# An mLSTM cell with a GELU block: three products of the cell as pairs of 64-column halves of the array

## The chip, the cores and the metric

The kernel runs on one core of a Trainium2 chip. The metric is the time of one execution on the device in microseconds (us), as the median of several runs. TensorE (PE in the profile) multiplies, its weight loads have a row of their own (PEld); VectorE is DVE, ScalarE is ACT, GpSimd is POOL, and SP issues the transfers.

## What is computed

A gated recurrent cell over 768 tokens for 4 batches of 8 heads, with keys, values and queries 40 wide, and behind it a feed-forward block with an exact GELU on all 3072 tokens. Everything is float32 except the two weight matrices, which come in float64.

```python
def _attn_ref(q, k, v, i_gate, f_gate, o_gate):      # (4, 8, 768, 40), gates (4, 8, 768)
    for t in range(S):
        m_new = np.maximum(f_gate[:, :, t] + m, i_gate[:, :, t])
        f_stab = np.exp(f_gate[:, :, t] + m - m_new)
        i_stab = np.exp(i_gate[:, :, t] - m_new)
        m = m_new
        C = f_stab[:, :, None, None] * C + i_stab[:, :, None, None] * np.einsum('bhd,bhe->bhde', vt, kt)
        n = f_stab[:, :, None] * n + i_stab[:, :, None] * kt
        h_tilde = np.einsum('bhde,bhe->bhd', C, qt)
        nq = np.einsum('bhd,bhd->bh', n, qt)[:, :, None]
        y[:, :, t] = 1.0 / (1.0 + np.exp(-o_gate[:, :, t])) * h_tilde / np.maximum(np.abs(nq), 1.0)

def _moe_ref(x, w_in, w_out):                        # x = y as (3072, 320), w_in (320, 2048), w_out (2048, 320)
    h = x @ w_in
    return 0.5 * h * (1.0 + erf(h / sqrt(2))) @ w_out
```

## The kernel before

The cell runs in six chunks of 128 tokens. Within a chunk the recurrence becomes products of matrices; a state (C with n as its 41st column) is carried from chunk to chunk. All the work of a chunk is done for each of the four batches b in turn, and one token lies on each partition.

The parts of the cell for one batch are four functions in `cell_steps`. `turn` (L268) transposes keys and queries, two heads at a time, into `pt` and copies them to `kT` and `qT`. Each of these holds pairs of heads: the first head of a pair in partitions 0 to 63, the second in 64 to 127. `scores` (L278) multiplies keys and queries of every head into `ps`, with the two heads of a pair in the two row halves of the array, and VectorE multiplies that by the weights W. From chunk 1 on it then reads the state: `pf` (L293) is one product for each of four pairs of heads, with `qT` (128 by 128 tokens) as the loaded operand and the state of the pair (82 columns) streamed. The state of a pair is block diagonal, so that one product serves both heads. VectorE scales it into `far`. Up to chunk 4 `scores` also updates the state: GpSimd weights the values (`vw`, L300), `pc` (L305) is one product for each pair with the keys of both heads loaded (128 columns) and the weighted values of both streamed (82 columns). Of its four blocks, head by head, only the two on the diagonal are used; GpSimd decays the state (L314) and VectorE adds those two blocks (L315). `values` (L317) multiplies W of each of eight heads (128 by 128, loaded) by its values and a column of ones (41, streamed) into `ph` (L321), adds `far`, and gates and divides the result on GpSimd and VectorE. `turn_y` (L337) transposes that through `px` into `xT`; its third transpose loads 64 columns.

The feed-forward block follows for all four batches of the chunk together: `up_steps` (L353) makes 16 pieces `pu` of 512 tokens, each from three products with 128, 128 and 64 rows, and `down_steps` (L363) sums 16 products into `po` for each batch.

The order of work on each engine is the order of the calls. `weave` spreads one list of steps between another. In chunk 0 the cell is woven with the conversion of `w_in` from float64 (ScalarE, GpSimd, VectorE); the up projection of chunk 0 is woven with that of `w_out`. Every later cell is woven with the down projection of the chunk before, four products of `po` after each step; the up projections stand alone. `activations` (exponentials and sigmoids on ScalarE) come ahead of each cell. The three products `pf`, `pc` and `ph` share two PSUM banks in turn (`ps_h`).

In the trace each float32 product appears as two weight loads and two matmuls, a transpose as one of each.

Of the kernel before, what the change touches and what calls it, by code (L numbers as in the profile page):

```python
# [9 lines left out]
F32 = mybir.dt.float32  # L10
U32 = mybir.dt.uint32
AF = mybir.ActivationFunctionType
OP = mybir.AluOpType

P = 128


# The upper halves of the float64 2^-126 and of the largest below 2^128, read as float32.
TINY = 3.4332275390625e-05
HUGE = 122879.9921875  # L20


def weave(main, fill):
    """Run the steps of main in order with those of fill spread evenly between them."""
    done = 0
    for n, step in enumerate(main):
        step()
        upto = len(fill) * (n + 1) // len(main)
        for f in fill[done:upto]:
            f()  # L30
        done = upto
    for f in fill[done:]:
        f()
# [3 lines left out]
def kernel(  # L37
# [9 lines left out]
    moe_w_out: bass.AP,  # L47
    out: bass.AP,
):
    # The cell in chunks of L tokens. With b_t the sum of f from the chunk's first token to t and  # L50
    # a_s = i_s - b_s, the stabiliser is m_t = b_t + M_t, M_t = max(m before the chunk, a_s for s <= t), and
    #   (C_t, n_t) = exp(m_before - M_t) (C, n)_before + sum over s <= t of exp(a_s - M_t) (v_s, 1) k_s^T.
    # Every exponent is at most 0, so this holds for gates of any size.
    nc = tc.nc

    B, H, S, D = q.shape
    L = P
    NCH = S // L
    NP = H // 2
    D1 = D + 1  # L60
# [23 lines left out]
    gates = gate_ctx.enter_context(tc.tile_pool(name="gates", bufs=1))  # L84
    ctx.enter_context(tc.manual_schedule())

    # ---- what stays: weights, state, load buffers with their constant parts
    w_in = const.tile([P, 3, DFF], F32, name="w_in")
    w_out = const.tile([P, NF, DM], F32, name="w_out")
    ident = const.tile([P, P], F32, name="ident")  # L90
# [13 lines left out]
    M_d = dram.tile([BH, S], F32, name="M_d")  # L104

    def load(n):
        """The inputs of token tile n (chunk n // B of batch n % B), one token a partition."""
        if n >= NCH * B:
            return
        c, b = divmod(n, B)  # L110
        for src, dst in ((q, qb), (k, kb), (v, vb), (o_gate, ob)):
            nc.sync.dma_start(out=dst[n % NLD][:, :, 0:D],
                              in_=src[b, :, c * L:(c + 1) * L, :].rearrange("h p d -> p h d"))
# [1 line left out]
    Mb, W = {}, {}  # L115

    def load_M(n):
        """M of token tile n on every partition."""
        if n >= NCH * B:
            return  # L120
        c, b = divmod(n, B)
        Mb[n] = wts.tile([P, H, L], F32, name="Mb", tag="Mb", bufs=NM)
        nc.sync.dma_start(out=Mb[n], in_=M_d[b * H:(b + 1) * H, c * L:(c + 1) * L]
                          .unsqueeze(0).to_broadcast([P, H, L]))
# [17 lines left out]
    for n in range(B):  # L142
        load(n)

    # ---- the gates, one row a head
    keep = gates.tile([BH, NCH, L], F32, name="keep")
    bl = gates.tile([BH, NCH, L], F32, name="bl")
    a = gates.tile([BH, NCH, L], F32, name="a")
# [34 lines left out]
    gate_ctx.close()  # L183
    gp = ctx.enter_context(tc.tile_pool(name="gp", bufs=1))

    # ---- the weights come in float64: the nearest float32, from the bits
    w_src = {}
    for name, w in (("in", moe_w_in), ("out", moe_w_out)):
        rows, cols = w.shape
# [1 line left out]
                              ap=[[2 * cols, rows], [1, 2 * cols]])  # L191

    def weight_steps():
        """What brings w_in and w_out in, a piece of at most WP columns a step."""
        pieces = []
        for f0 in range(0, DFF, WP):
            for cc, w in enumerate((P, P, KX)):
                pieces.append((w_src["in"][cc * P:cc * P + w, 2 * f0:2 * f0 + 2 * WP], w_in[0:w, cc, f0:f0 + WP]))
        n_in = len(pieces)
        for f in range(NF):  # L200
            pieces.append((w_src["out"][f * P:(f + 1) * P, :], w_out[:, f, :]))
        loaded = {}

        def fetch(i):
            if i < len(pieces):
                src, dst = pieces[i]
                w, n = dst.shape
                t = raw.tile([P, WP, 2], U32, name="bits", tag="bits")
                loaded[i] = t[0:w, 0:n, :]
                nc.sync.dma_start(out=loaded[i].rearrange("p n two -> p (n two)"), in_=src)  # L210

        def convert(i):
            dst = pieces[i][1]
            w, n = dst.shape
            x = loaded.pop(i)
            lo, hi = x[:, :, 0], x[:, :, 1]
            hf = hi.bitcast(F32)
            s = raw.tile([P, WP], F32, name="sig", tag="sig")[0:w, 0:n]
            p = raw.tile([P, WP], F32, name="pow", tag="pow")[0:w, 0:n]
            su, pu = s.bitcast(U32), p.bitcast(U32)  # L220
            # Into the range of float32: 0 below 2^-126, the end of the range from 2^128 on.
            nc.scalar.activation(out=s, in_=hf, func=AF.Abs)  # L222
            nc.gpsimd.tensor_scalar(out=s, in0=s, scalar1=TINY, scalar2=None, op0=OP.is_ge)  # L223
            nc.gpsimd.tensor_tensor(out=s, in0=s, in1=hf, op=OP.mult)  # L224
            nc.gpsimd.tensor_scalar(out=s, in0=s, scalar1=-HUGE, scalar2=HUGE, op0=OP.max, op1=OP.min)  # L225
            # The sign and the power of two, and the 53 bits of the significand rounded to 24.
            nc.vector.tensor_scalar(out=pu, in0=su, scalar1=3, scalar2=0x3F800000,  # L227
                                    op0=OP.logical_shift_left, op1=OP.bitwise_and)
            nc.vector.scalar_tensor_tensor(out=pu, in0=su, scalar=0xC0000000, in1=pu,
                                           op0=OP.bitwise_and, op1=OP.bitwise_or)  # L230
            nc.vector.tensor_scalar(out=su, in0=su, scalar1=0xFFFFF, scalar2=0x100000,
                                    op0=OP.bitwise_and, op1=OP.bitwise_or)
            nc.vector.scalar_tensor_tensor(out=s, in0=lo, scalar=2.0 ** -32, in1=su, op0=OP.mult, op1=OP.add)
            nc.vector.scalar_tensor_tensor(out=dst, in0=s, scalar=2.0 ** -20, in1=p, op0=OP.mult, op1=OP.mult)
            fetch(i + 2)

        fetch(0)
        fetch(1)
        steps = [lambda i=i: convert(i) for i in range(len(pieces))]
        return steps[:n_in], steps[n_in:]  # L240

    # ---- the cell
    def per_head(t, c, b):
        return t[:, c, b * H:(b + 1) * H].unsqueeze(2)

    def distances(c):
        """M_t - a_s for the chunk's weights exp(a_s - M_t); beyond the diagonal, what gives 0."""
        for b in range(B):
            n = c * B + b
            W[n] = wts.tile([P, H, L], F32, name="W", tag="W")  # L250
# [13 lines left out]

    def cell_steps(c):
        qT, kT, Pm, far, ys = {}, {}, {}, {}, {}

        def turn(b):  # L268
            n = c * B + b
# [8 lines left out]
        def scores(b):  # L278
            n = c * B + b
            Pm[b] = W.pop(n)  # L280
            # The heads of a pair run side by side in the array: each has its own bank.
            ps = [ps_sc.tile([P, NP, L], F32, name="ps", tag="sc") for hip in range(2)]
            for p in range(NP):
                for hip in range(2):
# [2 lines left out]
            for hip in range(2):  # L287
                w = Pm[b].rearrange("p (m two) t -> p m two t", two=2)[:, :, hip, :]
                nc.vector.tensor_tensor(out=w, in0=ps[hip], in1=w, op=OP.mult)  # L289
            if c > 0:  # L290
                pf = ps_h.tile([P, H, D1], F32, name="pf", tag="h")
                for p in range(NP):
                    nc.tensor.matmul(pf[:, 2 * p:2 * p + 2, :].rearrange("p h d -> p (h d)"), qT[b][:, p, :],  # L293
                                     state[b][:, p, :], start=True, stop=True)
                far[b] = two.tile([P, H, D1], F32, name="far", tag="far")
                nc.vector.tensor_tensor(out=far[b], in0=pf, in1=per_head(gT, c - 1, b).to_broadcast([P, H, D1]),
                                        op=OP.mult)
            if c + 1 < NCH:
                vw = two.tile([P, H, D1], F32, name="vw", tag="vw")
                nc.gpsimd.tensor_tensor(out=vw, in0=vb[n % NLD], in1=per_head(ewT, c, b).to_broadcast([P, H, D1]),  # L300
                                        op=OP.mult)
                pc = ps_h.tile([P, NP, 2 * D1], F32, name="pc", tag="h")
                for p in range(NP):
                    m = slice(2 * p, 2 * p + 2)
                    nc.tensor.matmul(pc[:, p, :], kb[n % NLD][:, m, :].rearrange("p h d -> p (h d)"),  # L305
                                     vw[:, m, :].rearrange("p h d -> p (h d)"), start=True, stop=True)
                for hip in range(2):
                    r, m = slice(DP * hip, DP * hip + DP), slice(D1 * hip, D1 * hip + D1)
                    st = state[b][r, :, m]
                    if c == 0:  # L310
                        nc.vector.tensor_copy(out=st, in_=pc[r, :, m])
                    else:
                        d = dec[r, c - 1, b * H:(b + 1) * H].rearrange("p (m two) -> p m two", two=2)[:, :, hip:hip + 1]
                        nc.gpsimd.tensor_tensor(out=st, in0=st, in1=d.to_broadcast([DP, NP, D1]), op=OP.mult)  # L314
                        nc.vector.tensor_tensor(out=st, in0=st, in1=pc[r, :, m], op=OP.add)  # L315

        def values(b):  # L317
            n = c * B + b
            ph = ps_h.tile([P, H, D1], F32, name="ph", tag="h")
            for h in range(H):  # L320
                nc.tensor.matmul(ph[:, h, :], Pm[b][:, h, :], vb[n % NLD][:, h, :], start=True, stop=True)  # L321
            hs = two.tile([P, H, D1], F32, name="hs", tag="hs")
            if c > 0:
                nc.vector.tensor_tensor(out=hs, in0=ph, in1=far[b], op=OP.add)  # L324
# [24 lines left out]
                    steps.append(lambda f=f, b=t - lag: f(b))  # L349
        return steps  # L350

    # ---- the feed-forward block, on the tokens of one chunk of every batch
    def up_steps(g):  # L353
        def step(f):
            m = slice(f * P, (f + 1) * P)
# [69 lines left out]
```

## Time and profile before

| what | value |
|---|---|
| time, median of 3 runs (lowest to highest) | 833.14 us (832.2 to 833.54) |
| span of the profiled execution, first to last instruction | 830.5 us |
| TensorE busy with matmuls | 674.7 us (81%) |
| weight loads | 394.8 us (48%) |
| VectorE busy | 240.7 us (29%) |
| GpSimd busy | 199.5 us (24%) |
| ScalarE busy | 170.4 us (21%) |

The profile gives the span of its execution alone; its whole time is not among the three runs, whose median lies 2.6 us above the span. Busy times overlap between engines. A busy TensorE is counted from the start of a matmul to its modelled end, so a stream of short matmuls looks busy while it waits for weight loads; how far the starts lie apart tells more.

### The profile page before, as it was taken

How to read it: one execution, taken by the hardware profiler on the slowest of the kernel's cores; microseconds unless marked ns; L12 is line 12 of the kernel's file. 1: busy time of each engine (PE TensorE's matmuls, PEld its weight loads, DVE VectorE, ACT ScalarE, POOL GpSimd, SP SyncE). 2: the span in 40 equal slices, each digit the busy share in tenths (PEclk: the TensorE clock that was granted, in tenths of full speed). 3: DMA queues.
4: the chain of work that ended last, by engine and by line, in shares of the span. 5: the costliest groups of instructions: out<-in, count | busy, mean ns of one | idle time of the engine just before them, and what ended most of it. 6: DMA issues, size and time to landing. Idle time of an engine off the chain costs nothing.

```text
span 830.5 us, 7094 instructions
## 1 busy us (share of the span) xinstructions
PE 674.7 (81%) x2714; PEld 394.8 (48%) x2714; DVE 240.7 (29%) x438; ACT 170.4 (21%) x288; POOL 199.5 (24%) x214
## 2 busy tenths in 40 slices
PE   2136424477579999799999799997999997999998
PEld 1125321122258733388533587333885335773365
DVE  4257554455534320034400144200344001330000
ACT  1411002111330022510223300225102234012200
POOL 2276654766612130011300021300113000000000
PEclk9975556788879999999999899998999998999999
DMA  9944371522204540024500035400221000000000
GB/s 141 248 80 95 66 120 29 148 64 63 63 9 66 79 110 0 0 41 66 133 23 1 6 64 82 109 0 1 41 40 41 1 0 9 9 17 0 0 9 24
DMA packets 132208, 43.47 MB, mean 52 GB/s; under 512 B 101104, under 2 KB 128752, under 8 KB 132176
## 3 DMA queue, kind: packets, MB, share of 16 engines
q1 hardware_dynamic: 132176, 43.04, 25.7%
q8 instruction: 21, 0.34, 0.2%
q14 instruction: 11, 0.09, 0.0%
HBM read 38.99 MB, written 4.03 MB: 52 GB/s over the span
## 4 chain that ended last, share of the span: by engine, by line
PE 67%; POOL 13%; issue 11%; ACT 5%; DVE 1%; DMA 1%; SPq 0%; POOLq 0%; ACTq 0%
PE pu L358 28%; PE po L371 25%; POOL sig L225 4%; PE ph L321 4%; POOL sig L223 4%; POOL sig L224 3%; PE ps L286 3%; PE pf L293 3%; ACT W L260 2%; PE pt L273 2%; PE pc L305 2%; POOL W L253 1%; ACT ob L263 1%; PE px L341 1%; ACT L263 1%
## 5 line engine op out<-in xcount | busy, mean ns | idle before, releaser
L358 PE MATMUL pu<-xT,w_in 128*128 128x512 f32 (+1 forms) x576 | 296.2, 646 | 36.4 <-ACT g L359 20.8
L371 PE MATMUL po<-w_out,g 128*128 128x320 f32 x768 | 228.5, 445 | 0.0
L358 PEld LDWEIGHTS pu<-xT,w_in 128*128 128x128 f32 (+1 forms) x576 | 96.6, 193 | 233.2 <-issue 189.8
L371 PEld LDWEIGHTS po<-w_out,g 128*128 128x128 f32 x768 | 143.6, 196 | 51.2 <-issue 5.0
L289 DVE TENSOR_TENSOR W<-ps,W 128x512 f32<-128x512 f32 x48 | 30.9, 685 | 293.5 <-PE ps L286 293.5
L359 ACT ACTIVATE g<-pu 128x512 f32<-128x512 f32 x96 | 57.1, 594 | 187.2 <-PE pu L358 187.2
L314 POOL TENSOR_TENSOR state<-state,dec 64x164 f32<-64x164 f32 x32 | 14.7, 461 | 241.5 <-PE pf L293 240.3
L273 PE MATMUL pt<-ident,kb 128*128 128x128 f32 x96 | 19.2, 335 | 60.5 <-ACT kT L276 60.5
L328 POOL TENSOR_TENSOR y<-hs,ob 128x320 f32<-128x320 f32 x24 | 19.3, 805 | 189.0 <-DVE hs L324 164.8
L321 PEld LDWEIGHTS ph<-vb,W 128*128 128x128 f32 x384 | 53.0, 215 | 4.0 <-PE px L341 0.8
L321 PE MATMUL ph<-vb,W 128*128 128x41 f32 x384 | 51.7, 300 | 0.4 <-PE px L341 0.4
L305 PE MATMUL pc<-vw,kb 128*128 128x82 f32 x160 | 24.9, 306 | 32.2 <-POOL vw L300 32.2
L253 POOL TENSOR_SCALAR_AFFINE_SELECT W<-W 128x1024 f32<-128x1024 f32 x24 | 37.2, 1571 | 56.9 <-DVE W L251 56.9
L273 PEld LDWEIGHTS pt<-ident,kb 128*128 128x128 f32 x96 | 14.1, 173 | 69.3 <-ACT kT L276 63.5
L223 POOL TENSOR_SCALAR sig<-sig 128x320 f32<-128x320 f32 (+2 forms) x28 | 34.8, 1243 | 47.0 <-ACT sig L222 47.0
L225 POOL TENSOR_SCALAR sig<-sig 128x320 f32<-128x320 f32 (+2 forms) x28 | 44.3, 1582 | 2.5
L251 DVE TENSOR_TENSOR W<-Mb,aT 128x1024 f32<-128x1024 f32 x24 | 33.3, 1425 | 26.0 <-DMA Mb<-M_d 26.0
L227 DVE TENSOR_SCALAR pow<-sig 128x320 uint32<-128x320 uint32 (+2 forms) x28 | 15.2, 543 | 86.3 <-POOL sig L225 86.2
L305 PEld LDWEIGHTS pc<-vw,kb 128*128 128x128 f32 x160 | 22.7, 219 | 33.3 <-POOL vw L300 33.3
L374 ACT COPY o_sb<-po 128x320 f32<-128x320 f32 x24 | 10.2, 425 | 132.3 <-PE po L371 132.3
L276 ACT COPY kT<-pt 128x512 f32<-128x512 f32 x24 | 13.9, 579 | 106.5 <-PE pt L273 106.5
L222 ACT ACTIVATE sig<-bits 128x320 f32<-128x320 f32 (+2 forms) x28 | 15.6, 563 | 97.4 <-DMA bits<-in_moe_w_out_dram 66.3
(71 smaller groups left out, 453.9 us busy)
## 6 DMA issues: line engine op xcount, KB each, us to landing
Mb<-M_d SPq DMA_DIRECT2D x24, 512.0 KB, 5.3
bits<-in_moe_w_out_dram SPq DMA_DIRECT2D x16, 320.0 KB, 2.9
bits<-in_moe_w_in_dram SPq DMA_DIRECT2D x8, 512.0 KB, 3.8
qb<-in_q_dram SPq DMA_DIRECT2D x24, 160.0 KB, 4.1
kb<-in_k_dram SPq DMA_DIRECT2D x24, 160.0 KB, 4.2
vb<-in_v_dram SPq DMA_DIRECT2D x24, 160.0 KB, 4.2
ob<-in_o_gate_dram SPq DMA_DIRECT2D x24, 160.0 KB, 3.8
out_dram<-o_sb SPq DMA_DIRECT2D x24, 160.0 KB, 1.9
```

What stands on the lines that cost most here:

```text
L223: nc.gpsimd.tensor_scalar(out=s, in0=s, scalar1=TINY, scalar2=None, op0=OP.is_ge)
L224: nc.gpsimd.tensor_tensor(out=s, in0=s, in1=hf, op=OP.mult)
L225: nc.gpsimd.tensor_scalar(out=s, in0=s, scalar1=-HUGE, scalar2=HUGE, op0=OP.max, op1=OP.min)
L251: nc.vector.tensor_tensor(out=W[n], in0=Mb.pop(n), in1=per_head(aT, c, b).to_broadcast([P, H, L]), op=OP.subtract)
L253: nc.gpsimd.affine_select(out=W[n], in_=W[n], compare_op=OP.is_ge, fill=1.0e4, base=0, pattern=[[0, H], [1, L]], channel_multiplier=-1)
L273: nc.tensor.transpose(pt[:, p, :], src[n % NLD][:, 2 * p:2 * p + 2, :].rearrange("p h d -> p (h d)"), ident)
L289: nc.vector.tensor_tensor(out=w, in0=ps[hip], in1=w, op=OP.mult)
L305: nc.tensor.matmul(pc[:, p, :], kb[n % NLD][:, m, :].rearrange("p h d -> p (h d)"), vw[:, m, :].rearrange("p h d -> p (h d)"), start=True, ...
L321: nc.tensor.matmul(ph[:, h, :], Pm[b][:, h, :], vb[n % NLD][:, h, :], start=True, stop=True)
L358: nc.tensor.matmul(pu, w_in[0:w, cc, m], xT[0:w, cc, :], start=(cc == 0), stop=(cc == 2))
L359: nc.scalar.activation(out=g[:, f, :], in_=pu, func=AF.Gelu)
L371: nc.tensor.matmul(po, g[:, f, b * L:(b + 1) * L], w_out[:, f, :], start=(f == 0), stop=(f == NF - 1))
```

## The change

The three products of the cell that load 128 columns are cut into halves of 64 columns. In the array each half has columns of its own, 0 to 63 or 64 to 127, and writes the same half of the partitions of its bank.

- `ph` (values): for each head two products, one for the first 64 tokens and one for the last 64; both stream the same 41 columns of values.
- `pf` (state read): for each pair of heads two products in the same way; both stream the same 82 columns of the state.
- `pc` (state update): for each pair one product a head, with the keys of that head loaded (64 columns) and the values of that head streamed (41 columns). The two blocks off the diagonal are no longer made, and the tile has 41 columns instead of 82.

The copies and sums that read `pc` read the whole half instead of a slice. Comments are left out below; the rest of the kernel is the same, five lines further down at the end.

```diff
@@ -264,6 +264,7 @@

     def cell_steps(c):
         qT, kT, Pm, far, ys = {}, {}, {}, {}, {}
+        halves = (slice(0, DP), slice(DP, P))

         def turn(b):
             n = c * B + b
@@ -278,7 +279,7 @@
         def scores(b):
             n = c * B + b
             Pm[b] = W.pop(n)
...
             ps = [ps_sc.tile([P, NP, L], F32, name="ps", tag="sc") for hip in range(2)]
             for p in range(NP):
                 for hip in range(2):
@@ -288,10 +289,12 @@
                 w = Pm[b].rearrange("p (m two) t -> p m two t", two=2)[:, :, hip, :]
                 nc.vector.tensor_tensor(out=w, in0=ps[hip], in1=w, op=OP.mult)
             if c > 0:
+
                 pf = ps_h.tile([P, H, D1], F32, name="pf", tag="h")
                 for p in range(NP):
-                    nc.tensor.matmul(pf[:, 2 * p:2 * p + 2, :].rearrange("p h d -> p (h d)"), qT[b][:, p, :],
-                                     state[b][:, p, :], start=True, stop=True)
+                    for r in halves:
+                        nc.tensor.matmul(pf[r, 2 * p:2 * p + 2, :].rearrange("p h d -> p (h d)"), qT[b][:, p, r],
+                                         state[b][:, p, :], start=True, stop=True)
                 far[b] = two.tile([P, H, D1], F32, name="far", tag="far")
                 nc.vector.tensor_tensor(out=far[b], in0=pf, in1=per_head(gT, c - 1, b).to_broadcast([P, H, D1]),
                                         op=OP.mult)
@@ -299,26 +302,28 @@
                 vw = two.tile([P, H, D1], F32, name="vw", tag="vw")
                 nc.gpsimd.tensor_tensor(out=vw, in0=vb[n % NLD], in1=per_head(ewT, c, b).to_broadcast([P, H, D1]),
                                         op=OP.mult)
-                pc = ps_h.tile([P, NP, 2 * D1], F32, name="pc", tag="h")
+
+                pc = ps_h.tile([P, NP, D1], F32, name="pc", tag="h")
                 for p in range(NP):
-                    m = slice(2 * p, 2 * p + 2)
-                    nc.tensor.matmul(pc[:, p, :], kb[n % NLD][:, m, :].rearrange("p h d -> p (h d)"),
-                                     vw[:, m, :].rearrange("p h d -> p (h d)"), start=True, stop=True)
+                    for hip in range(2):
+                        nc.tensor.matmul(pc[halves[hip], p, :], kb[n % NLD][:, 2 * p + hip, :], vw[:, 2 * p + hip, :],
+                                         start=True, stop=True)
                 for hip in range(2):
-                    r, m = slice(DP * hip, DP * hip + DP), slice(D1 * hip, D1 * hip + D1)
+                    r, m = halves[hip], slice(D1 * hip, D1 * hip + D1)
                     st = state[b][r, :, m]
                     if c == 0:
-                        nc.vector.tensor_copy(out=st, in_=pc[r, :, m])
+                        nc.vector.tensor_copy(out=st, in_=pc[r])
                     else:
                         d = dec[r, c - 1, b * H:(b + 1) * H].rearrange("p (m two) -> p m two", two=2)[:, :, hip:hip + 1]
                         nc.gpsimd.tensor_tensor(out=st, in0=st, in1=d.to_broadcast([DP, NP, D1]), op=OP.mult)
-                        nc.vector.tensor_tensor(out=st, in0=st, in1=pc[r, :, m], op=OP.add)
+                        nc.vector.tensor_tensor(out=st, in0=st, in1=pc[r], op=OP.add)

         def values(b):
             n = c * B + b
             ph = ps_h.tile([P, H, D1], F32, name="ph", tag="h")
             for h in range(H):
-                nc.tensor.matmul(ph[:, h, :], Pm[b][:, h, :], vb[n % NLD][:, h, :], start=True, stop=True)
+                for r in halves:
+                    nc.tensor.matmul(ph[r, h, :], Pm[b][:, h, r], vb[n % NLD][:, h, :], start=True, stop=True)
             hs = two.tile([P, H, D1], F32, name="hs", tag="hs")
             if c > 0:
                 nc.vector.tensor_tensor(out=hs, in0=ph, in1=far[b], op=OP.add)
```

On TensorE, one batch of chunk 1 from the scores to the values. `state_99` and `kb_113` are the state and the keys of a batch, `vb_118` the values of the one before. Before:

```order
L286 MATMUL ps<-qT,kT 128x128 x8
L293 MATMUL pf<-state_99,qT 128x82 x4
L305 MATMUL pc<-vw,kb_113 128x82 x4
L371 MATMUL po<-w_out,g 128x320 x4
L321 MATMUL ph<-vb_118,W 128x41 x8
L371 MATMUL po<-w_out,g 128x320 x4
```

And with the change:

```order
L287 MATMUL ps<-qT,kT 128x128 x8
L296 MATMUL pf<-state_99,qT 64x82 x8
L309 MATMUL pc<-vw,kb_113 64x41 x8
L376 MATMUL po<-w_out,g 128x320 x4
L326 MATMUL ph<-vb_118,W 64x41 x16
L376 MATMUL po<-w_out,g 128x320 x4
```

Nothing changes its place; each of the three groups has twice as many products that fill half the partitions. The instructions of the other engines stand in the same order with the same waits.

## Rows read from the trace of the kernel before

**Rows 1.** The page: the span, and each engine's busy time, share of span and instructions.

```profile
span 830.5 us, 7094 instructions
...
PE 674.7 (81%) x2714; PEld 394.8 (48%) x2714; DVE 240.7 (29%) x438; ACT 170.4 (21%) x288; POOL 199.5 (24%) x214
```

**Rows 2.** Windows over the five stages of cell and down projection: length, busy time (instructions).

```profile
core 0: us, PE busy (x) PEld busy (x) DVE busy (x) ACT busy (x) POOL busy (x), PEclk, DMA share, GB/s
219.19:291.46 72.27, 58.15 (x348) 46.07 (x349) 28.84 (x62) 16.05 (x28) 16.36 (x23) 0.91 0.31 53
342.07:405.20 63.13, 57.09 (x350) 45.49 (x350) 21.44 (x46) 12.07 (x23) 9.36 (x16) 0.97 0.31 50
...
sum 323.55, PE 285.27 PEld 225.78 DVE 110.01 ACT 64.33 POOL 47.65; mean PE 57.05 PEld 45.16 DVE 22.00 ACT 12.87 POOL 9.53
```

**Rows 3.** Who TensorE waited for: us in total, times, longest us.

```profile
PE pt L273 <- ACT kT L276: 60.5, 6, 22.2
PE pc L305 <- POOL vw L300: 32.2, 4, 12.0
```

**Rows 4.** Chain that ended last, from 246 to 256 us: start us, us, what.

```profile
247.22 1.09 PE ps L286 x16
248.31 1.05 PE pf L293 x8
249.36 0.89 PE pc L305 x8
250.25 2.19 PE po L371 x8
252.44 1.71 PE ph L321 x16
```

**Rows 5.** Groups by form from 348.12 to 405.20 us, matmuls: busy us, mean ns, idle us.

```profile
L321 PE MATMUL ph<-vb,W 128*128 128x41 f32 x64 | 7.5, 277 | 0.0
...
L293 PE MATMUL pf<-state,qT 128*128 128x82 f32 x32 | 4.5, 283 | 0.0
L305 PE MATMUL pc<-vw,kb 128*128 128x82 f32 x32 | 4.2, 275 | 0.0
```

**Rows 6.** The same stretch, weight loads (PEld).

```profile
L321 PEld LDWEIGHTS ph<-vb,W 128*128 128x128 f32 x64 | 7.8, 192 | 0.6
...
L341 PEld LDWEIGHTS px<-ident,y 128*128 128x128 f32 x8 | 1.1, 141 | 0.8
L341 PEld LDWEIGHTS px<-ident,y 128*64 128x64 f32 x4 | 0.4, 110 | 0.0
```

**Rows 7.** Timeline from 318.0 to 321.1 us: start us, us, engine, what, idle before.

```profile
318.06 0.30 PEld L358 LDWEIGHTS pu<-xT,w_in 128*128 128x128 f32 x2 [0.76 <-issue]
...
318.59 0.19 PEld L358 LDWEIGHTS pu<-xT,w_in 128*128 128x128 f32 x1 [0.24 <-issue]
319.02 0.19 PEld L358 LDWEIGHTS pu<-xT,w_in 128*128 128x128 f32 x1 [0.24 <-issue]
319.97 0.29 PEld L358 LDWEIGHTS pu<-xT,w_in 64*128 64x128 f32 x2 [0.76 <-issue]
321.02 0.19 PEld L358 LDWEIGHTS pu<-xT,w_in 128*128 128x128 f32 x1 [0.76 <-issue]
```

**Rows 8.** Timeline from 361.0 to 368.2 us, one batch of chunk 2.

```profile
360.88 1.16 PE L286 MATMUL ps<-qT,kT 64*128 64x128 f32 x16
...
362.14 1.29 DVE L289 TENSOR_TENSOR W<-ps,W 128x512 f32<-128x512 f32 x2 [5.63 <-PE ps L286]
...
363.35 0.49 DVE L296 TENSOR_TENSOR far<-pf,gT 128x328 f32<-128x328 f32 x1
...
364.09 0.68 DVE L315 TENSOR_TENSOR state<-state,pc 64x164 f32<-64x164 f32 x2 [0.26 <-PE pc L305]
...
366.01 1.88 PE L321 MATMUL ph<-vb,W 128*128 128x41 f32 x16
```

## The prediction

> **What bounds the kernel now.** I read first the page's busy times: over the span of 830.5 us TensorE is busy for 674.7, no other engine for more than 240.7 [rows 1]. A share over the whole span hides stages, so next the windows by stage. In the five stages in which the cell of a chunk is woven with the down projection of the chunk before (chunks 1 to 5), TensorE is busy for 285.27 of 323.55 us [rows 2]. What it waits for there is the head of each stage: the first copy of kT after the activations, 6 waits in all, 60.5 us [rows 3]. Behind that head no changed group has any idle time before it: values (ph), state read (pf) and state update (pc) all show 0.0 us [rows 5]. So in chunks 1 to 5 a microsecond taken off TensorE inside the stage comes off the end. In chunk 0 it does not: TensorE waits there for GpSimd, 32.2 us before pc in four waits [rows 3], and what it saves it waits longer. I count chunk 0 at nothing; its cover is that wait.
>
> What bounds TensorE in the three groups is read from their pitch. Every fp32 product is recorded as two loads and two matmuls. In the chain, 8 records of pc take 0.89 us and 16 of ph 1.71 [rows 4], 111 and 107 ns each, although pc streams 82 columns and ph only 41. Eight records of po with 320 columns take 2.19 us [rows 4], 0.85 ns a column, which makes 35 ns for 41 columns and 70 for 82. The pitch is thus not the stream's: it is the same for both widths, and it is the load of 128 weight columns, which runs one behind the other (PEld busy 7.8 us for ph where the matmuls show 7.5 [rows 5, 6]).
>
> **The change part by part.** No engine but TensorE gets another instruction, another order or another wait; the copies, products and sums on VectorE and GpSimd have the shapes they had. TensorE's products of the three groups double in number and halve in weight columns; pc also halves its streamed columns to 41, which lay under its load anyway.
>
> *Price of a half load.* The only row with a load of 64 columns is the third transpose of px: 110 ns against 141 for 128 columns [rows 6], 31 ns less. A transpose is recorded as one load, and an ordinary load of 128 columns takes 192 ns, 51 more than the transpose's [rows 6], so its part that grows with columns is some 1.7 to 2 times as long: a half load is worth 51 to 62 ns off a pitch of 111. I take 58 ns for the pitch of half loads; the ends are 49 and, if only the transpose's 31 ns come off, 80.
>
> *Do two halves run side by side?* No row of before has two column halves in the array. The nearest is ps, whose two heads lie in the two row halves: 16 records with 128 columns loaded and 128 streamed take 1.09 us, a change of mode included [rows 4], under 70 ns each where one alone would need 107 or more (ph). There the halves do run together. I take the same for column halves, so a pair costs what one costs: 58 ns for ph and pc, where the load is longer than the stream (35 ns), and 70 ns for pf, where the stream of 82 columns is. If the halves take turns, a pair costs 116 ns, and 140 for pf.
>
> *Change of mode.* The up projection's third piece has 64 rows, so it goes from full array to row halves and back each time. One round goes from 318.06 to 321.02 us, 2.96 us for six records; two records in one mode lie 0.43 apart (318.59 to 319.02) [rows 7]. Six of these are 2.58, and 0.38 remain for two changes: 0.19 each. The other end is 0, since a change between column widths might not drain the array. I take 0.19, the row that is nearest. After the change ph is entered and left in another mode (2 changes, 0.38 us a batch). The block of scores already leaves ps by a change (pf's 1.05 us hold it: 0.16 over 8 times 111 ns [rows 4]); that now leads into pf's mode, and one more, 0.19, stands between pc (pf in chunk 5) and po.
>
> The Trainium skill, "TensorEngine Tiling (Array Packing)", Tiling Modes, states of both points that a change of mode drains TensorE and that tiles load and multiply in parallel. The trace agrees with the drain in [rows 7] and with the parallel run in [rows 4], for row halves alone; of column halves no row of before shows either.
>
> *Sum per batch, chunks 1 to 4.* ph: 1.71 becomes 16 x 0.058 + 0.38 = 1.31, 0.40 us less. pf: 8 x 0.111 = 0.89 becomes 8 x 0.070 = 0.56, 0.33 less. pc: 0.89 becomes 8 x 0.058 = 0.46, 0.43 less. The added change: 0.19 more. Together 0.97 us less, for 16 batches 15.5 us. In chunk 5 pc is missing: 0.40 + 0.33 - 0.19 = 0.54, for 4 batches 2.2 us. **Sum 17.7 us**, so the profiled span of 830.5 becomes 812.8. The median of the runs, 833.1, lies 2.6 us over the span, which stays; 815.4.
>
> *What is late next.* The values wait for VectorE's second product of W, which ends at 362.14 + 1.29 = 363.43; ph begins at 366.01 [rows 8], 2.58 us later. The changed block before it gets 0.57 us shorter, so 2.0 us of cover stay. ph also takes over the bank of pf, free at 363.84, when far is done, and the next pf that of pc, free when the two state sums end at 364.77 [rows 8]; both with more than a microsecond to spare. If this cover failed, each late piece would cost its lateness 20 times, so half a microsecond would take 10 of the 17.7 us.
>
> **The rivals.**
> *The halves take turns.* One mechanism: the array takes one column half's load at a time. ph then costs 16 x 0.116 + 0.38 = 2.24, 0.53 more than now; pf 8 x 0.140 = 1.12, 0.23 more; pc 0.93, 0.04 more; with 0.19 that is 0.99 a batch, 15.8 us for 16 batches, and 0.95 x 4 = 3.8 in chunk 5: slower by 19.6, 853 us. It decides from a pitch of the pair on: now a batch has 1.71 + 0.89 + 0.89 = 3.49 us, less 0.57 for changes of mode leaves 2.92 for 32 pairs, so over 91 ns a pair the change loses. For it: no row shows column halves together, and both halves stream the same rows of memory. Against it: the row halves of ps, whose loads do not wait for each other. The Trainium skill has a rule that would bring this about: by "TensorE: Matmul & The Clock Gate", Part 3, a load overlaps matmuls in flight only where the row groups differ, and two column halves share all their rows. For the full array the trace does not bear it out: the loads of ph and its matmuls are both busy nearly all of the group's time [rows 5, 6].
>
> *Half loads are as long as whole ones*, though side by side: ph 16 x 0.111 + 0.38 = 2.16, 0.45 more, pf and pc as now, 0.19 more: 0.64 x 20 = 12.8, 846 us. Against it the 110 of 141 ns of px.
>
> *Changes between column widths are free:* three fewer of 0.19 in each of 20 batches, 11.4 us more gain, 804 us. *Half of the gain:* a pair staggered, or half loads at 80 ns: 24 pairs x 0.022 + 8 x 0.010 = 0.61 a batch less, and 0.43 in chunk 5, 11.5 us: 827 us.
>
> *It doesn't do what it says:* the "only useful blocks" of the update save nothing on their own, since VectorE and GpSimd read as many elements as before and the stream lay under the load. That is in the sum already.
>
> **How the numbers follow.** What a measurement of this kernel can tell from no change is some 0.2%, 1.7 us. Chances: side by side with half loads near 58 ns and a change of mode at up to 0.19 us, 801 to 822 us: 0.66; of this the forecast, **815 us**. A part of the gain, 822 to 831: 0.10. Within 1.7 us of 833: 0.04. Loads not shorter, 838 to 846: 0.05. Turns, 846 to 854: 0.13. Under 801: 0.02. Faster is 0.78, same 0.04, slower 0.18. The range takes the first two and the third, **801 to 835**: 0.80.
>
> **What would show it.** In the page of after TensorE's 2714 records become 3418 (the 704 of the three groups stand twice). In the chain ph is x32 at about 0.93 us, pf x16 about 0.56 and pc x16 about 0.46, beside a po after them that holds the change. The loads of ph with 64 columns show some 140 ns instead of 192. The stage of 63.13 us [rows 2] is about 3.9 shorter, the waits for kT stay as they are, and no new wait of TensorE for W, far or the state stands in the list. Starts of two ph records about 58 ns apart one by one, or a ph x32 of 1.9 us, would show turns. A gain in chunk 0, or a wait that grows by what a stage saves, would show that the bound was read wrongly.

## The result, and the profile after

The changed kernel takes 809.3 us (median of four runs, 807.8 to 811.0) where the kernel before takes 832.9 in the same session: a ratio of 0.972, with an interval of 0.971 to 0.974. That is 23.6 us less; forecast were 17.7 less, 815 us, in a range of 801 to 835. The profiled execution went from a span of 830.5 to 806.0 us.

The page of after, span and busy times; it answers to [rows 1]:

```profile
span 806.0 us, 8502 instructions
...
PE 644.6 (80%) x3418; PEld 356.3 (44%) x3418; DVE 239.3 (30%) x438; ACT 170.7 (21%) x288; POOL 199.7 (25%) x214
```

TensorE has the 704 records more that were announced, and is busy 30 us less; the other engines do what they did.

The chain that ended last in the changed kernel, for one batch of chunk 2 with the po ahead of it (start us, us, what); it answers to [rows 4]:

```profile
352.19 2.15 PE po L376 x8
354.34 1.09 PE ps L287 x16
355.44 0.72 PE pf L296 x16
356.16 0.44 PE pc L309 x16
356.60 2.35 PE po L376 x8
358.95 1.06 PE ph L326 x32
360.02 2.35 PE po L376 x8
```

In the kernel before, the po behind the values reads so in the same view:

```profile
367.89 2.23 PE po L371 x8
```

Each stretch has to be read with the po behind it, since a pause at its end shows in the record that follows: a po takes 2.15 us behind full-array records, 2.23 behind the old ph and 2.35 behind a group in halves. Values: 1.71 + 2.23 = 3.94 us before [rows 4], now 1.06 + 2.35 = 3.41, which is **0.53 us less**. State read and update: 1.05 + 0.89 + 2.19 = 4.13 before [rows 4], now 0.72 + 0.44 + 2.35 = 3.51, **0.62 us less**. ps takes 1.09 us in both.

Groups by form in one stage (341.86 to 394.62 us) of the changed kernel, matmuls, which answer to [rows 5], then the weight loads of ph, which answer to [rows 6] (busy us, mean ns, idle before):

```profile
L326 PE MATMUL ph<-vb,W 128*64 128x41 f32 x128 | 4.5, 231 | 0.0
L296 PE MATMUL pf<-state,qT 128*64 128x82 f32 x64 | 3.2, 240 | 0.0
L309 PE MATMUL pc<-vw,kb 128*64 128x41 f32 x64 | 2.5, 225 | 0.0
```

```profile
L326 PEld LDWEIGHTS ph<-vb,W 128*64 128x64 f32 x128 | 4.1, 138 | 1.8 <-issue 1.8
```

A half load of ph takes 138 ns where a whole one took 192, 54 less; the pitch of pc, from start to start, went from 111 ns a record to 56 ns a pair, as eight pairs in 0.44 to 0.45 us show. There are twice as many records, and the group of ph is busy 4.5 us a stage instead of 7.5. All three still show no idle time before them: TensorE sets the pace as before.

The five stages of cell and down projection, from the first transpose after the wait for kT to the first record of the up projection, with TensorE's granted clock (PEclk); first before (four of the five stages and the sum), then after:

```profile
233.31:291.46 58.15, 58.15 (x348) 0.96 0.34 55
348.12:405.20 57.08, 57.08 (x349) 0.98 0.34 56
461.85:520.08 58.23, 58.23 (x349) 0.96 0.34 54
...
690.50:745.18 54.68, 54.68 (x317) 0.95 0.03 10
sum 285.26, PE 285.25; mean PE 57.05
```

```profile
232.26:285.21 52.95, 52.95 (x477) 0.97 0.38 60
341.86:394.62 52.76, 52.76 (x476) 0.97 0.37 61
451.28:503.94 52.66, 52.66 (x476) 0.97 0.38 60
...
669.87:720.69 50.82, 50.82 (x413) 0.97 0.03 11
sum 261.81, PE 261.80; mean PE 52.36
```

Together they are 23.45 us shorter. Length times granted clock is the same for stages of the same work: 58.15 x 0.96, 57.08 x 0.98 and 58.23 x 0.96 make 55.8 to 55.9 before, 52.95 and 52.76 x 0.97 make 51.2 to 51.4 after. So stages of one kernel differ in how long they run at 1.2 GHz after TensorE has waited for kT: in windows of 2 us from the start of the stage of chunk 2, PEclk reads 0.50, 0.81 and 1.00 before and 0.50, 0.68 and 1.00 after. The work of a stage became 4.6 us shorter.

Whom TensorE waited for in the changed kernel, the lines that answer to [rows 3]:

```profile
PE pt L274 <- ACT kT L277: 58.7, 6, 22.2
PE pc L309 <- POOL vw L303: 36.3, 4, 14.0
```

The wait for kT is 1.8 us less in sum, that for vw in chunk 0 is 4.1 us more: nearly all that TensorE saved in chunk 0 it waited for GpSimd.

### The profile page after: what moved, and what is told of

It is laid out like the page before. It is cut to its first block, busy times and chain, and to the rows that moved or that the text cites. A ratio compares the mean times of both kernels' runs of the same rounds, so it can differ in the third digit from the quotient of the medians.

```text
span 806.0 us, 8502 instructions
## 1 busy us (share of the span) xinstructions
PE 644.6 (80%) x3418; PEld 356.3 (44%) x3418; DVE 239.3 (30%) x438; ACT 170.7 (21%) x288; POOL 199.7 (25%) x214
## 4 chain that ended last, share of the span: by engine, by line
PE 66%; POOL 14%; issue 12%; ACT 6%; DVE 1%; DMA 0%; POOLq 0%; ACTq 0%; SPq 0%
PE pu L363 29%; PE po L376 26%; POOL sig L225 4%; POOL sig L223 4%; POOL sig L224 3%; PE ps L287 3%; PE ph L326 3%; ACT W L260 2%; PE pt L274 2%; PE pf L296 2%; POOL W L253 1%; ACT ob L263 1%; PE pc L309 1%; PE px L346 1%; ACT L263 1%
## 5 line engine op out<-in xcount | busy, mean ns | idle before, releaser
L309 PE MATMUL pc<-vw,kb 128*64 128x41 f32 x320 | 14.1, 242 | 36.3 <-POOL vw L303 36.3
L287 PE MATMUL ps<-qT,kT 64*128 64x128 f32 x384 | 31.6, 303 | 2.2 <-DVE W L290 2.2
L326 PEld LDWEIGHTS ph<-vb,W 128*64 128x64 f32 x768 | 27.6, 152 | 12.0 <-issue 12.0
L326 PE MATMUL ph<-vb,W 128*64 128x41 f32 x768 | 30.3, 244 | 2.8 <-issue 2.8
```

What stands on the lines that cost most here:

```text
L287: nc.tensor.matmul(ps[hip][:, p, :], kT[b][r, p, :], qT[b][r, p, :], start=True, stop=True)
L326: nc.tensor.matmul(ph[r, h, :], Pm[b][:, h, r], vb[n % NLD][:, h, :], start=True, stop=True)
```

## The experiments

My theory was that pairs of halves run at once, at the price of a half load (58 ns), and that each change of mode (of the array's shape, from one record to the next) costs 0.165 us (from the stretches above: ph is 1.06 - 16 x 0.058 = 0.13 over its pairs, the po behind it 2.35 - 2.15 = 0.20 over its own time). The rivals were that shorter loads alone pay, that the update's useful blocks pay, and that the pauses counted as changes of mode are something else.

**One part alone: the values.** The kernel before, and of the change only this:

```diff
-                nc.tensor.matmul(ph[:, h, :], Pm[b][:, h, :], vb[n % NLD][:, h, :], start=True, stop=True)
+                for r in halves:
+                    nc.tensor.matmul(ph[r, h, :], Pm[b][:, h, r], vb[n % NLD][:, h, :], start=True, stop=True)
```

> Only the values (ph) in column halves; pf and pc as in the kernel before. Theory (pairs run side by side at 58 ns, two changes of mode a batch at 0.165 us): the stretch of ph takes 0.53 us less a batch, 20 batches, 10.5 us: 822.4 us. Rival (the gain is that of pc's useful blocks and the rest is neutral): no change, 833 us.

Measured: 821.7 us (ratio to before 0.988, 0.986 to 0.990). In the chain:

```profile
363.40 1.06 PE ph L323 x32
364.46 2.35 PE po L373 x8
```

The stretch is the changed kernel's, 1.06 and 2.35 us. The values alone bring 10.7 of the 23.6 us, as the theory had it.

**One part alone: the state read.** The kernel before, and only this:

```diff
-                    nc.tensor.matmul(pf[:, 2 * p:2 * p + 2, :].rearrange("p h d -> p (h d)"), qT[b][:, p, :],
-                                     state[b][:, p, :], start=True, stop=True)
+                    for r in halves:
+                        nc.tensor.matmul(pf[r, 2 * p:2 * p + 2, :].rearrange("p h d -> p (h d)"), qT[b][:, p, r],
+                                         state[b][:, p, :], start=True, stop=True)
```

> Only the state read (pf) in column halves. Theory: 8 records of 111 ns become 8 pairs of 65 (0.37 us), less one more change of mode a batch (0.165): 0.20 us, 20 batches, 4.1 us: 828.8 us. If a change between full and half column width costs nothing by itself: 7.4 us, 825.5 us.

Measured: 828.5 us (0.996, 0.995 to 0.998). In the chain, pf and the whole-array pc behind it:

```profile
373.05 0.72 PE pf L295 x16
373.77 1.05 PE pc L307 x8
```

pf takes 0.33 us less than in [rows 4] (eight pairs of 70 ns and the change of 0.16 ahead of them; the expectation had 65), and pc, which now follows a change of mode, 0.16 more. So the change between full and half column width has its price: it is not free by itself.

**One part alone: the state update.** The kernel before, and only this; the two sums then read pc[r]:

```diff
-                    m = slice(2 * p, 2 * p + 2)
-                    nc.tensor.matmul(pc[:, p, :], kb[n % NLD][:, m, :].rearrange("p h d -> p (h d)"),
-                                     vw[:, m, :].rearrange("p h d -> p (h d)"), start=True, stop=True)
+                    for hip in range(2):
+                        nc.tensor.matmul(pc[halves[hip], p, :], kb[n % NLD][:, 2 * p + hip, :], vw[:, 2 * p + hip, :],
+                                         start=True, stop=True)
```

> Only the state update (pc) in column halves, only its useful blocks. Theory: 8 records of 111 ns become 8 pairs of 58 (0.43 us), less two more changes of mode a batch (0.33): 0.10 us, 16 batches, 1.6 us: 831.3 us. Rival (useful blocks are what pays): 0.43 us and more a batch, 7 us or more: 826 us or less.

Measured: 829.2 us (0.997, 0.995 to 0.998), 3.2 us less than before, where the theory had 1.6 and the rival 7 or more. In the chain:

```profile
371.97 1.05 PE pf L294 x8
373.02 0.60 PE pc L306 x16
373.61 2.35 PE po L372 x8
```

0.89 + 2.19 us of [rows 4] became 0.60 + 2.35: 0.13 us less a batch, 2.1 us for the 16 batches that update. That is between the two: the price of a change is a little under 0.165. The rest, 1.1 us, is no more than these runs differ among themselves. The useful blocks do not pay by themselves; most of what pc saves goes to the two changes around it.

Added up, the three parts alone give 10.7 + 3.9 + 3.2 = 17.8 us, the whole change 23.6. The difference is in the neighbourhood: pf and pc side by side need one change of mode where each alone needs one and two, 0.3 us a batch less, 5 us.

**The same work in another order: halves apart.** The changed kernel, with the loops of the values exchanged:

```diff
-            for h in range(H):
-                for r in halves:
+            for r in halves:
+                for h in range(H):
```

> The changed kernel with one other order: of the values of a batch, first the first halves of all eight heads, then the second halves. Loads, streams and changes of mode are the same. Theory (the gain is that two neighbouring halves run at once): 32 records at 58 ns instead of 16 pairs, 0.93 us more a batch, 20 batches, 18.6 us above the changed kernel: 828 us. Rival (shorter loads alone make the gain, or TensorE finds the pairs far apart): as the changed kernel, 809 us.

Measured: 826.3 us, 17.0 us above the changed kernel (ratio to before 0.993, 0.991 to 0.995). In the chain the values take 1.78 us instead of 1.06:

```profile
362.18 1.78 PE ph L326 x32
363.96 2.35 PE po L376 x8
```

Loads, streams and changes of mode are the same as in the changed kernel, so shorter loads alone do not make the gain: **two halves at once do.** The loss is 0.72 us a batch, though, not 0.93: 14.4 of the 17.0 us in 20 batches. The rest goes with the clock, which in the windows of the five stages reads 0.96 here and 0.97 in the changed kernel. Records of ph that touch a window of 0.16 us, in this run at the start, the middle and the end of one stretch, and then in the changed kernel:

```profile
374.20:374.36 0.16, 0.16 (x6) 1.00 0.00 0
374.62:374.78 0.16, 0.16 (x10) 1.00 0.00 0
375.10:375.26 0.16, 0.16 (x6) 1.00 0.00 0
```

```profile
359.10:359.26 0.16, 0.16 (x13) 1.00 0.00 0
359.30:359.46 0.16, 0.16 (x14) 1.00 0.00 0
```

6 records touch a window while one half is alone, 13 or 14 in the changed kernel, and 10 in the middle of the stretch: there the end of the first halves and the beginning of the second run at once. (0.93 - 0.72) / 0.058 makes some four pairs that still met.

**How far apart may they be?** The changed kernel, with the values ordered by two heads:

```diff
-            for h in range(H):
-                for r in halves:
+            for h0 in range(0, H, 2):
+                for r in halves:
+                    for h in range(h0, h0 + 2):
```

> The changed kernel, the values of a batch ordered by two heads: the first halves of two heads (4 records), then their second halves (4 records), and so on. Theory after the run with the halves apart (a half is started beside another as long as it lies no more than 4 records further on): all pairs still meet, the stretch of ph stays at 1.26 us over its neighbours, 809 us. Rival (only direct neighbours run together): half of the pairs are lost, 0.47 us a batch, 818 us.

Measured: 809.4 us, as the changed kernel. In the chain:

```profile
360.16 1.08 PE ph L327 x32
```

With four records of one half ahead of the other's, all pairs still meet: TensorE began the records of the second half beside the first ones, ahead of their place in the program. The trace does not name the half of a record, so this is read from the length of the stretch. With sixteen, some four met.

**What the useful blocks give.** The changed kernel, with the update streaming both heads' values again:

```diff
-                        nc.tensor.matmul(pc[halves[hip], p, :], kb[n % NLD][:, 2 * p + hip, :], vw[:, 2 * p + hip, :],
+                        nc.tensor.matmul(pc[halves[hip], p, :], kb[n % NLD][:, 2 * p + hip, :],
+                                         vw[:, 2 * p:2 * p + 2, :].rearrange("p h d -> p (h d)"),
...
-                pc = ps_h.tile([P, NP, D1], F32, name="pc", tag="h")
+                pc = ps_h.tile([P, NP, 2 * D1], F32, name="pc", tag="h")
```

> The changed kernel, but each half of pc streams the weighted values of both heads (82 columns), as before; the two sums read their blocks out of it. Theory (the load hides the stream up to some 58 ns): a pair goes from 58 to 65 ns as pf's, 0.06 us a batch, 16 batches, 0.9 us: 810 us. Rival (the useful blocks alone are a good part of the gain): 0.3 us a batch and more, 814 us or more.

Measured: 813.4 us, 4.1 above the changed kernel. In the chain:

```profile
351.27 0.57 PE pc L309 x16
```

pc takes 0.57 instead of 0.44 to 0.45 us: a pair goes to 71 ns, which is the stream of 82 columns at 0.85 ns each. That is 0.12 us a batch, 1.9 us in all, twice what the theory had. The other 2 us are not in the product. The five stages, of which the longest and the sum stand here, show where they lie:

```profile
564.18:618.66 54.48, 54.48 (x476) 0.95 0.20 34
sum 266.41, PE 266.40; mean PE 53.28
```

That is 4.6 us more than the 261.81 of the changed kernel, and PEclk reads 0.95 to 0.97 where it read 0.97 throughout: what the product does not explain was lost to the clock. So the smaller blocks are worth some 2 of the 23.6 us, and only because the loads beside them had become short.

**A change of mode taken away elsewhere.** If a change costs near 0.2 us, the third piece of the up projection, which has 64 rows, should be cheaper with 128. The changed kernel, with zeros in the upper rows:

```diff
+    nc.vector.memset(w_in[KX:P, 2, :], 0.0)
+    nc.vector.memset(xT[KX:P, 2, :], 0.0)
...
-                nc.tensor.matmul(pu, w_in[0:w, cc, m], xT[0:w, cc, :], start=(cc == 0), stop=(cc == 2))
+                nc.tensor.matmul(pu, w_in[:, cc, m], xT[:, cc, :], start=(cc == 0), stop=(cc == 2))
```

> The changed kernel, and the up projection's third piece over all 128 rows: the upper 64 rows of the weights and of xT's third part are set to zero once, so that no change of mode is left there. Theory (a change costs 0.165 to 0.2 us wherever TensorE sets the pace): a round of six records goes from 2.96 to 2.57 us, 0.39 x 16 x 5 = 31 us in the up projections of chunks 1 to 5, nothing in chunk 0: 778 us. Rival (the pauses are not the change of mode but belong to the 64-row records or to the bank that changes): 809 us.

Measured: 781.4 us (ratio to before 0.939, 0.937 to 0.940), and 780.8 when it ran again. Weight loads of the up projection (start us, us), which answer to [rows 7], and the up projection in the chain:

```profile
317.98 0.19 PEld L365 LDWEIGHTS pu<-xT,w_in 128*128 128x128 f32 x1 [0.24 <-issue]
318.40 0.19 PEld L365 LDWEIGHTS pu<-xT,w_in 128*128 128x128 f32 x1 [0.24 <-issue]
...
320.55 0.19 PEld L365 LDWEIGHTS pu<-xT,w_in 128*128 128x128 f32 x1 [0.24 <-issue]
```

```profile
286.81 41.21 PE pu L365 x96
```

A round of six records takes 317.98 to 320.55 = 2.57 us where it took 2.96 [rows 7]: the loads now lie 0.42 to 0.43 apart throughout. The 96 records take 41.2 us, where the chain of the kernel before has pieces of 47.28 us:

```profile
291.62 47.28 PE pu L358 x96
```

The changed kernel's are as long, so over five chunks this is 30.4 us. The time fell by 28.0: in this trace the five stages of cell and down projection, whose work is the same, came out 3.1 us longer (264.89 for 261.81 us), at a PEclk of 0.94 to 0.97. So the pauses were not the bank's, which still changes every round; they went with the piece of 64 rows. That records of 64 rows pause by themselves is unlikely, since those of ps run at under 70 ns each [rows 4]; the change of mode is what is left, by exclusion. This kernel beats both of the case by a wide margin, for multiplications with zeros.

**Two changes less in the cell.** The values of a batch between the next one's scores and state read would spare two changes for three batches of four. To the kernel with the third piece over all rows is added, vw being made at the start of scores:

```diff
+            if between is not None:
+                values(between)
             if c > 0:
                 pf = ps_h.tile([P, H, D1], F32, name="pf", tag="h")
...
+                if c > 0 and f is scores and 1 <= t - lag < B:
+                    steps.append(lambda b=t - lag: scores(b, b - 1))
+                elif c > 0 and f is values and 0 <= t - lag < B - 1:
+                    continue
```

> As the kernel with the third piece over all rows, and from chunk 1 on the values of a batch come between the scores and the state read of the next one, so that ph, pf and pc follow each other in one mode (for three of four batches two changes less); the weighted values vw are made ahead of that. Theory: 3 x 2 x 5 changes of 0.165 us, 5 us less than that kernel: 773 us. Rival (pc waits for the bank that hs frees, or px for y): what it waits, as much as it gains, 778 us or more.

Measured: 779.9 us, 1.5 less than that kernel instead of 5. The chain, and in the timeline the reader of ph's bank and pc:

```profile
350.53 1.06 PE ph L330 x32
351.60 0.59 PE pf L304 x16
352.19 0.10 issue
352.29 0.67 PE pc L313 x16
```

```profile
351.64 0.50 DVE L333 TENSOR_TENSOR hs<-ph,far 128x328 f32<-128x328 f32 x1 [6.37 <-PE ph L330]
...
352.29 0.67 PE L313 MATMUL pc<-vw,kb 128*64 128x41 f32 x16
```

pf is 0.13 us shorter, since it follows ph in the same mode, but pc is 0.23 longer and has 0.10 us of waiting ahead of it. It takes the bank that ph had two tiles before, and hs reads that until 351.64 + 0.50 = 352.14; pc begins at 352.29. The rival was right: the wait took what the two changes gave. Chunk 5, which has no pc, shows that they were there to win: its stage takes 50.20 us at PEclk 0.96, that of the kernel without the new order 52.26 at 0.94, so length times clock is some 0.9 us less, about what three batches of 0.33 make.

So the order was turned: pf first, then the values of the batch before, pc, and the scores last. pc then takes the bank of pf, and far empties it while ph runs. In the code `score` holds ps and the products with W; vw at the start of `scores` and the list of steps are as in the run before:

```diff
+            if c == 0:
+                score()
             if c > 0:
                 pf = ps_h.tile([P, H, D1], F32, name="pf", tag="h")
...
+            if between is not None:
+                values(between)
             if c + 1 < NCH:
                 pc = ps_h.tile([P, NP, D1], F32, name="pc", tag="h")
...
+            if c > 0:
+                score()
```

> As the kernel with the third piece over all rows, but from chunk 1 on a batch goes state read (pf), values of the batch before (ph), state update (pc), scores (ps), so that pc takes the bank that far frees while ph runs, and two changes of mode fall away for three of four batches without a wait. Theory: 0.32 x 3 x 5 = 4.8 us less than that kernel, 776.6 us, and in chunks 1 to 4 the stage is 0.96 us shorter at the same clock. Rival (another wait takes the place: W is late for the values, since VectorE makes it after hs, y and the state): as that kernel, 781 us.

Measured: 774.1 us (ratio to before 0.930, 0.928 to 0.931). The same kernel in the old order ran beside it:

> The kernel with the third piece over all rows once more, beside the other order on the same chip: 781 us.

That one took 780.8 us, so the order is worth 6.7 us, of which the theory has 4.8. In the windows the five stages are 7.3 us shorter together (259.02 for 266.35 us) and length times granted clock some 5; the rest is clock, 0.95 to 0.97 for 0.94 to 0.97. In the chain nothing waits:

```profile
348.38 0.72 PE pf L306 x16
349.10 0.91 PE ph L336 x32
350.01 0.47 PE pc L317 x16
350.48 1.09 PE ps L294 x16
```

ph takes 0.91 us, 16 pairs of 57 ns with no change of mode in it, pc 0.47. It is the fastest of the versions run here.

## Why the prediction was right

*What bounds the kernel.* Right. In chunks 1 to 5 what came off TensorE came off the span, and nearly all it saved in chunk 0 went to its wait for vw. The first up projection began 0.5 us earlier and the stage of chunk 1 1.05 us earlier than before; I had counted nothing there. Whether the 1.05 us belong to the change is not shown: the same kernel, run twice with the third piece over all rows, begins that stage at 233.33 and at 232.18 us.

*Half loads at 58 ns, side by side.* Right: 56 to 58 ns a pair, forecast from the row halves of ps as the only model for two halves at once, and px for the length of half a load. The rival of turns, which had 116 ns a pair, is shown wrong by that and by the run with the halves apart, where the order alone cost 0.72 us a batch. Two column halves share their rows, and 13 or 14 records of them touch 0.16 us where 6 of one half do. The rule named in that rival (TensorE: Matmul & The Clock Gate, Part 3, in the Trainium skill: a load overlaps matmuls in flight only with other row groups) says otherwise; the measurement decides. The other page of the Trainium skill that was cited, TensorEngine Tiling (Array Packing), Tiling Modes, has tiles that load and multiply in parallel, as these pairs do, and a drain at each change of mode, which the pauses of 0.13 to 0.20 us fit.

*Changes of mode at 0.19 us.* Right in kind, a little high. Two of them around ph cost 0.33 us.

*The sum.* It was 6 us short, and the step that was mis-sized is the first term. I took ph's old time as 1.71 us, but the po behind it took 2.23 us instead of 2.15, which belongs to it, so it was 1.79. With changes at 0.165 the values give 0.53 a batch, not 0.40: 2.6 us in 20 batches. pf and pc give 0.62, not 0.57, in 16 batches: 0.8. In chunk 5 pf gives (1.05 + 2.19) - (0.72 + 2.35) = 0.17, not 0.14. Together the cell has 20 x 0.53 + 16 x 0.62 + 4 x 0.17 = 21.2 us. The span lost 24.5: 1.05 more came before the stage of chunk 1, and some 2 us from the clock. From the windows, length times (1 - PEclk) is 2.3, 1.1, 2.3 and 2.7 us in the four stages shown before and 1.5 to 1.6 in those after. The stages of after began where less of them fell to 1.2 GHz; I see nothing in the change that sets this, but did not test it. The two executions of one kernel named above differ by 1.5 us in the sum of their five stages (264.89 and 266.35). So some 3.5 of the 6 us are the mis-sized terms, and the rest is not shown to be the change's.

*What is late next.* Right: TensorE's waits are the old ones. The order that joined the values to pf showed how thin such cover can be: there the bank that hs reads was free too late for pc.

*The useful blocks.* I had said that they save nothing. On the full array that holds, but beside half loads of 58 ns the stream of 82 columns shows, at 71: they are worth some 2 us.

## What to carry to other kernels

Where short matmuls lie as far apart as their weight loads last, cut the loaded columns in half and put the halves into the two column halves of the array, next to each other in the program. Then count the changes between array shapes, 0.13 to 0.2 us each here, and order or pad the products so that few are left: here that was worth more (35 us) than the halves (24). Read a stretch together with the record that follows it, where the pause at its end is booked. A difference of 2 or 3 us between two traces may be the clock alone, so read PEclk by stage before looking for another cause.

## What the runs showed of the hardware beyond what I had expected

By the lengths of the stretches, TensorE starts products of the other half of the array ahead of their place in the program: with four records of one half first all pairs still met (1.08 us for the values), with sixteen about four did (1.78 us instead of the 1.99 that no overlap would give).

Two identical stages differ by up to 1.2 us (57.08 and 58.23) by when the clock returns from 1.2 GHz after the wait ahead of them; length times granted clock agrees within 0.2 us.
